# Linear attention and a gated mixture of experts on one core: three copies of v and one clamp of k done by GpSimd

## The chip, the core and the metric

The kernel runs on one core of a Trainium2 chip. The metric is the device time of one execution in microseconds (us); less is better. Engines: TensorE (PE, matrix products and transposes; PEld is its weight load), VectorE (DVE), ScalarE (ACT), GpSimd (POOL) and SyncE (SP, which here only starts transfers). Each engine works its own instructions off in order, and semaphores order the engines against each other.

## The reference

Two stages, batch 8, 8 heads, 576 positions, head width 64 (so 512 model columns), 8 experts of width 1024:

```
phi(x) = where(x > 0, x, exp(x) - 1) + 1
q_p, k_p = phi(q), phi(k)
kv  = einsum('bhsd,bhse->bhde', k_p, v);  z = sum(k_p, over s)
out = einsum('bhsd,bhde->bhse', q_p, kv) / (einsum('bhsd,bhd->bhs', q_p, z) + 1e-6)
x   = out with the heads side by side                       # 8 x 576 x 512
logits = x @ w_gate;  local = sigmoid(x @ w_local)
for each batch, position by position:
    e = argmax(logits[s]) if s == 0 or local[s] < 0.5 else the previous position's e
    out[s] = softmax(logits[s])[e] * (relu(x[s] @ w1[e]) @ w2[e])
```

## The kernel before

**Tiling.** Each batch a is cut into two groups n = 2a, 2a + 1 of four heads. A group's k, q and v are tiles of 128 rows by 1152 floats (`kraw`, `qraw`, `vraw`; four, two and three buffers taken in turn). Positions lie 9 to a row; the first ninth is handled apart as the "last" slice.

**Steps of a group n.** `Lk.n`, `Lq.n`, `Lv.n` load (on SP's queue; for n = 0 and 1 v comes in two parts, `Lv.n` with 5 of the 9 columns and `Lv.n.1` with 4). `E.k.n` and `E.q.n` are the exponentials on ACT. phi of k is `min(max(k + 1, 1), exp(k))` for batch 0: `CL.n` is the clamp `max(k + 1, 1)` into a spare tile, `P.k.n` takes the minimum in DVE. phi of q is `E2.q.n` (relu, in place) and `P.q.n` (min and add, in two halves). `VC.n` and `VC.n.1` copy v into `vone`, which has a column of ones beside each 64 columns so that one product yields both kv and z. `K.n` and `K.n.1` are those products on PE, `KC.n` copies their result `kv` out of PSUM. `QL`/`Q` transpose q on PE, `QLC`/`QC` copy that out to `qT`. `NL`/`N` form numerators and denominators, `DL`/`D` divide on DVE into `xb`, `XL`/`X` transpose that, `XLC`/`XC` copy it to `xT`.

**Steps of a batch a.** `R.a.0` and `R.a.1` are the gate's logits, `PK`/`BK` pick the expert, `W.a.x` loads its weights (transfers started by POOL, since their address comes from the picked index), `H.a.m`/`HC` the hidden layer, `O.a.i`/`OC` the output, `ST` its store. The kernel assumes that one expert serves a whole batch; flags checked at the end start a general path if not (it does not run here).

**Order.** A single hand-written list, `ORDER`, sets the order for all engines: each engine's queue is that list, filtered to its own steps. A number behind a slash is the PSUM slot (`K.1/3` and `K.0/3` share one, so `K.0` needs `KC.1` done). A `^` sends a copy to the engine other than its default: the copies of v go to DVE by default, and with `^` to ACT. So before the change `VC.1`, `VC.1.1` and `VC.0` are ACT's, `VC.0.1` and both clamps DVE's. POOL has, at the start, a few memsets, the identity matrices (`ident`, `identb`) and two small loads; then nothing until `W.0.0`.

**Waits that matter here.** `Lq.2` overwrites the buffer that `P.q.0` reads, so SP holds it until `P.q.0` is done; `Lk.3`, `Lk.2`, `Lq.3` (which waits for `P.q.1`), `Lv.3` (which waits for `VC.0`) and `Lv.2` follow in SP's queue. The clamp of group 0 is put into `vraw[2]`, that of group 1 into `kraw[2]`. On ACT, `E.k.3` stands ahead of `XLC.0`.

Of the kernel before, what the change touches and what calls it, by code (L numbers as in the profile page):

```python
# [20 lines left out]


ORDER = """
Lq.0 Lk.1 FILL/0 Lv.1 Lv.1.1 Lv.0 Lk.0 Lq.1 Lv.0.1 E0.0 P0.0 E.k.1 CL.1 WT/1 E.q.0 P.k.1 QL.0/2 VC.1^
E2.q.0^ QLC.0 K.1/3 VC.1.1^ P.q.0.0 K.1.1 E.k.0 P.q.0 CL.0 Q.0/2 Lq.2 VC.0^ Lk.3 P.k.0 E.q.1 Lk.2 KC.1^
VC.0.1 QC.0 K.0/3 E2.q.1^ K.0.1 P.q.1.0 KC.0^ P.q.1 E.q.2 NL.0/2 N.0.0.1/3 DL.0 Lq.3 E.k.3 Lv.3 WG D.0.0.1
XL.0/2 Lv.2 Q.1/1 XLC.0^ R.0.0/2 QC.1 N.0.0.0/3 RC.0.0 D.0.0.0 W.0.0 E.k.2 N.0.1.1/2 N.0.1.0/1 PK.0 E2.k.3
D.0.1.1 E.q.3 D.0.1.0 BK.0 P.k.3 VC.3^ W.0.1 X.0.0/3 X.0.1/2 XC.0.0 XC.0.1^ K.3/1 E2.q.2^ E2.q.3^ R.0.1/3
# [47 lines left out]
def kernel(  # L76
# [11 lines left out]
    nc = tc.nc  # L88
    P = 128
    B, H, S, Dh = q.shape  # L90
    D = H * Dh
    E = moe_w_gate.shape[1]
# [28 lines left out]
    with ExitStack() as main:  # L121
# [7 lines left out]
        kraw = [raw.tile([P, 2, C, Dh], F32, name=f"kraw{i}") for i in range(NKR)]  # L129
# [71 lines left out]

        BK = 512
        got, other = {}, set()

        def bank(label, *name, dt=F32):
            i = got[name]
            ps = psp.tile([P, SLOTS[i], BK if dt == F32 else 2 * BK], dt, name=label, tag=f"ps{i}")
            ps = open_[name] = ps if size[name] == 2 else ps[:, 0, :]
            return ps
# [51 lines left out]
        def clamp(n):  # L261

            return (kraw[2] if n else vraw[2]).rearrange("p g c d -> p (g c d)")

        def clamp_k(n):
            nc.vector.tensor_scalar(clamp(n), kraw[n].rearrange("p g c d -> p (g c d)"), 1.0, 1.0,
                                    Alu.add, Alu.max)

        def phi(n, x, both=False, c0=0, c1=C, gs=(0, 1)):
# [18 lines left out]
        def on_act(*name, act=False):  # L288
            return (name in other) != act

        def copy(dst, src, *name, act=False):
            (nc.scalar.copy if on_act(*name, act=act) else nc.vector.tensor_copy)(dst, src)  # L292

        def v_ones(n, i=None):
            c0, c1 = (0, C) if i is None else CV[i:i + 2]
            dst, src = vone[n % 2][:, :, c0:c1, :Dh], vraw[n % NV][:, :, c0:c1, :]
            copy(dst, src, *(("VC", n) + ((i,) if i else ())))
# [11 lines left out]
        def kv_out(n):  # L309
            kv[n] = kvp.tile([P, 2, W], F32, name="kv")  # L310
            copy(kv[n], open_.pop(("K", n))[:, :, :W], "KC", n)
# [8 lines left out]
        def q_main_out(n):  # L320
            ps = open_.pop(("Q", n))
            for r in range(2):
                copy(qT[n][:, :, :SM].rearrange("q t (i p r) -> q r t i p", i=NC - 1, r=2)[:, r],
                     ps[:, r, :].rearrange("q (i t p) -> q t i p", i=NC - 1, t=2), "QC", n, act=True)
# [319 lines left out]
        for a in range(B):  # L644
            for j in range(NJ):
                n = a * NJ + j
# [7 lines left out]
                for x in "kq":  # L654
                    both = a > 0 or x == "q"
                    if not both:
                        op(("CL", n), lambda n=n: clamp_k(n))
                    c0 = int(a == 0 and x == "q")
                    if c0:
                        if n == 0:  # L660
                            op(("E0", n), exp0)
                            op(("P0", n), phi0)
                    op(("E", x, n), lambda n=n, x=x, c0=c0: exps(n, x, False, c0))
                    if both:
                        op(("E2", x, n), lambda n=n, x=x, c0=c0: relus(n, x, c0))
                    if c0:
                        op(("P", x, n, 0), lambda n=n: phi(n, "q", True, 1, C, (0,)))
                    op(("P", x, n),
                       lambda n=n, x=x, b=both, c0=c0: phi(n, x, b, c0, C, (1,) if c0 else (0, 1)))
# [59 lines left out]
        for word in ORDER.split():  # L729
            name, _, at = word.rstrip("^").partition("/")  # L730
            name = tuple(int(x) if x.isdigit() else x for x in name.split("."))
# [261 lines left out]
```

## Time and profile before

| | |
|---|---|
| time, median of 3 runs | 220.41 us (218.78 to 221.2) |
| the profiled execution's own time | 222.17 us |
| its span in the profile | 220.6 us |
| mean granted TensorE clock | 0.971 |
| busy: PE, DVE, ACT, POOL | 207.2 (94%), 177.8 (81%), 131.2 (59%), 13.6 us (6%) |
| chain that ended last, by engine | PE 87%, DMA 5%, DVE 2%, ACT 2%, issue 1% |

The profile is of one execution, and its times count from the start of the span; 1.57 us of the execution's time lie outside of it. The page cuts the span into 40 slices: there PE is at nine tenths or more in every slice from the sixth to the last but one, and lower in the first five; the DMA engines are at nine tenths or more in the slices 2 to 7. POOL is busy in slices 1 and 5 and after that only in short pieces.

### The profile page before, as it was taken

What the parts mean: (1) busy time and instruction counts of PE and PEld (TensorE: products, weight loads), DVE (VectorE), ACT (ScalarE), POOL (GpSimd) and SP (SyncE); (2) the same over time, 40 slices, a digit from 0 to 9 for tenths busy, and PEclk for the clock granted to TensorE, in tenths of its full rate; (3) what the DMA queues carried; (4) which work ended last, traced back from release to release, by engine and by line L of the source; (5) the groups of instructions that cost most, each with busy time, mean ns of one, the idle gap of its engine ahead of it and who ended that gap; (6) DMA issues with size and microseconds to landing.
All of it is one profiled execution on the core that took longest, in us unless ns stands there. A gap on an engine that the chain in (4) does not pass through costs nothing.

```text
span 220.6 us, 8567 instructions
## 1 busy us (share of the span) xinstructions
PE 207.2 (94%) x3702; PEld 152.7 (69%) x3715; DVE 177.8 (81%) x459; ACT 131.2 (59%) x197; POOL 13.6 (6%) x41
## 2 busy tenths in 40 slices
PE   7886699999999999999999999999999999999990
PEld 2575578767886698875888568874889578647640
DVE  0794987698999999999999989779897989586730
ACT  2678727599999999795248984483753302501120
POOL 4000500000010000210000000110000001100000
PEclk9978879999999999999999999999999999999997
DMA  5999999896976798999359979599230008998043
GB/s 192 369 307 341 166 195 216 270 371 222 360 249 260 236 378 235 370 228 195 67 154 332 304 232 333 97 183 155 77 146 3 4 15 324 189 197 255 3 153 97
DMA packets 24447, 46.77 MB, mean 212 GB/s; under 512 B 2124, under 2 KB 9808, under 8 KB 23508
## 3 DMA queue, kind: packets, MB, share of 16 engines
q1 hardware_dynamic: 16324, 37.49, 49.1%
q0 software_dynamic: 7392, 8.41, 24.0%
q8 instruction: 31, 0.51, 1.0%
q10 hardware_dynamic: 688, 0.26, 0.5%
q14 instruction: 12, 0.10, 0.1%
HBM read 61.88 MB, written 9.44 MB: 323 GB/s over the span
## 4 chain that ended last, share of the span: by engine, by line
PE 87%; DMA 5%; DVE 2%; ACT 2%; issue 1%; SPq 0%; DVEq 0%; ACTq 0%
PE hps L556 29%; PE yps L578 25%; PE kvps L306 9%; PE nps L357 7%; PE tq L317 6%; DMA kraw<-in_k_dram 5%; PE yps L582 4%; PE tx L391 3%; PE lps L433 2%; ACT ek L241 1%; PE npl L376 1%; PE lps L427 1%; PE tql L330 1%; DVE xb L345 1%; DVE kraw L274 1%
## 5 line engine op out<-in xcount | busy, mean ns | idle before, releaser
L556 PE MATMUL hps<-xT,w1cur 128*128 128x288 bf16 x512 | 67.8, 288 | 0.0
L578 PE MATMUL yps<-w2cur,hT 128*128 128x512 bf16 x243 | 58.4, 379 | 0.7
L556 PEld LDWEIGHTS <-w1cur 128*128 128x128 bf16 x512 | 49.1, 98 | 13.3 <-issue 0.6
L565 ACT ACTIVATE hT<-hps 128x576 bf16<-128x576 f32 x41 | 26.7, 657 | 37.7 <-PE hps L556 28.8
L578 PEld LDWEIGHTS <-hT 128*128 128x128 bf16 x256 | 24.0, 98 | 25.5 <-issue 0.3
L306 PE MATMUL kvps<-vone,kraw 64*64 64x65 f32 x1152 | 21.8, 229 | 2.0 <-ACT vone L292 1.0
L345 DVE TENSOR_TENSOR xb<-nps,rec 128x512 bf16<-128x512 f32 x32 | 22.1, 691 | 1.1
L281 DVE SCALAR_TENSOR_TENSOR fq<-fq,qraw 128x576 f32<-128x576 f32 (+1 forms) x32 | 22.4, 741 | 0.2
L306 PEld LDWEIGHTS kvps<-vone,kraw 64*64 64x64 f32 x1152 | 19.7, 143 | 3.6 <-ACT vone L292 1.5
L274 DVE SCALAR_TENSOR_TENSOR kraw<-ek,kraw 128x1152 f32<-128x1152 f32 x14 | 18.8, 1346 | 2.1 <-ACT kraw L248 2.1
L567 DVE TENSOR_SCALAR hT<-hps 128x576 bf16<-128x576 f32 x23 | 17.1, 752 | 4.2 <-PE hps L556 4.0
L357 PE MATMUL nps<-kv,qT 64*64 64x65 f32 x1024 | 20.3, 228 | 0.0
L241 ACT ACTIVATE fq<-qraw 128x1152 f32<-128x1152 f32 (+1 forms) x16 | 18.4, 1153 | 2.8 <-DMA qraw<-in_q_dram 2.8
L241 ACT ACTIVATE ek<-kraw 128x1152 f32<-128x1152 f32 x16 | 18.8, 1173 | 2.3 <-DMA kraw<-in_k_dram 2.3
L357 PEld LDWEIGHTS nps<-kv,qT 64*64 64x64 f32 x1024 | 18.2, 143 | 1.2 <-issue 0.5
L593 ACT ACTIVATE yo<-yps,pr 128x512 f32<-128x512 f32 x16 | 11.0, 690 | 11.3 <-PE yps L578 11.2
L317 PE MATMUL tq<-ident,fq 128*128 128x128 f32 x128 | 17.3, 280 | 0.0
L292 ACT COPY qT<-tq 128x512 f32<-128x512 f32 x28 | 15.9, 644 | 0.7 <-PE tq L317 0.6
L317 PEld LDWEIGHTS tq<-ident,fq 128*128 128x128 f32 x128 | 15.0, 145 | 0.8
L292 ACT COPY xT<-tx 128x1024 bf16<-128x1024 bf16 x9 | 9.1, 1014 | 10.7 <-PE tx L391 10.7
L595 DVE TENSOR_SCALAR yo<-yps,pr 128x512 f32<-128x512 f32 x16 | 11.7, 744 | 2.0 <-PE yps L578 1.9
L248 ACT ACTIVATE kraw<-kraw 128x1152 f32<-128x1152 f32 x10 | 11.7, 1169 | 0.0
(108 smaller groups left out, 218.5 us busy)
## 6 DMA issues: line engine op xcount, KB each, us to landing
kraw<-in_k_dram SPq DMA_DIRECT2D x16, 576.0 KB, 7.2
qraw<-in_q_dram SPq DMA_DIRECT2D x14, 576.0 KB, 5.3
vraw<-in_v_dram SPq DMA_DIRECT2D x14, 576.0 KB, 5.5
w1s<-in_moe_w_dram POOLq DMA_DIRECT2D x7, 1024.0 KB, 11.3
w2s<-in_moe_w_dram POOLq DMA_DIRECT2D x7, 1024.0 KB, 13.1
out_dram<-yo SPq DMA_DIRECT2D x14, 512.0 KB, 5.1
qraw<-in_q_dram SPq DMA_DIRECT2D x2, 512.0 KB, 4.0
w2cur<-in_moe_w_dram POOLq DMA_DIRECT2D x1, 1024.0 KB
```

The source lines that it names most:

```text
L241: nc.scalar.activation(e[:, :, c0:c1, :], raw_, Act.Exp)
L274: nc.vector.scalar_tensor_tensor(r, e, 1.0, r, Alu.min, Alu.add)
L281: nc.vector.scalar_tensor_tensor(e[:, g], e[:, g], 1.0, r[:, g], Alu.min, Alu.add)
L292: (nc.scalar.copy if on_act(*name, act=act) else nc.vector.tensor_copy)(dst, src)
L306: nc.tensor.matmul(ps[g * PH:(g + 1) * PH, t, :W], lhsT=f[h, g, c, :], rhs=vo[h, g, c, :], start=(c == 0), stop=(c == C - 1))
L317: nc.tensor.transpose(ps[:, r, i * P:(i + 1) * P], ex_[n, "q"][:, 1 + i + (NC - 1) * r, :, :], identity=ident)
L345: nc.vector.tensor_tensor(dst, ps[:, :, :, :Dh].rearrange("p g (i t) e -> p g i t e", t=2), rec.rearrange("p g (i t o) -> p g i t o", t=2, ...
L357: nc.tensor.matmul(ps[o * PH:(o + 1) * PH, g, (il * 2 + t) * W:(il * 2 + t + 1) * W], lhsT=qT[n][g * PH:(g + 1) * PH, t, i * P + o * PH:i ...
L556: nc.tensor.matmul(ps[:, u, :HS], lhsT=w1b[:, kk, m * P:(m + 1) * P], rhs=xT[b][:, kk, u * HS:(u + 1) * HS], start=(kk == 0), stop=(kk == ...
L565: nc.scalar.activation(dst, src, Act.Relu)
L567: nc.vector.tensor_scalar(dst, src, 0.0, None, Alu.max)
L578: nc.tensor.matmul(ps, lhsT=hT[b][:, m, i * P:(i + 1) * P], rhs=w2b[:, m, :], start=(m == 0), stop=(m == FK - 1))
```

## The change

Three of the four copies of v of batch 0 (`VC.1`, `VC.1.1`, `VC.0`) go from ACT to GpSimd, and the second clamp of batch 0 (`CL.0`, of k of group 0) from DVE to GpSimd. Their places in `ORDER` stay.

```
-... QL.0/2 VC.1^
-E2.q.0^ QLC.0 K.1/3 VC.1.1^ P.q.0.0 K.1.1 E.k.0 P.q.0 CL.0 Q.0/2 Lq.2 VC.0^ Lk.3 ...
+... QL.0/2 VC.1
+E2.q.0^ QLC.0 K.1/3 VC.1.1 P.q.0.0 K.1.1 E.k.0 P.q.0 CL.0 Q.0/2 Lq.2 VC.0 Lk.3 ...
...
+        on_pool = {("VC", 1), ("VC", 1, 1), ("VC", 0), ("CL", 0)}
...
         def clamp_k(n):
-            nc.vector.tensor_scalar(clamp(n), kraw[n].rearrange("p g c d -> p (g c d)"), 1.0, 1.0,
+            (nc.gpsimd if ("CL", n) in on_pool else nc.vector).tensor_scalar(clamp(n), kraw[n].rearrange("p g c d -> p (g c d)"), 1.0, 1.0,
                                     Alu.add, Alu.max)
...
         def copy(dst, src, *name, act=False):
-            (nc.scalar.copy if on_act(*name, act=act) else nc.vector.tensor_copy)(dst, src)
+            (nc.gpsimd.tensor_copy if name in on_pool else
+             nc.scalar.copy if on_act(*name, act=act) else nc.vector.tensor_copy)(dst, src)
```

ACT's queue at the start of batch 0, before. `vone_78<-vraw_75` are the two parts of `VC.1`, `vone_77<-vraw_74` is `VC.0`; `fq` is `E.q`, `ek` is `E.k`, `kv` is `KC.1`:

```order
L241 ACTIVATE ek<-kraw_69 128x1152
L241 ACTIVATE fq<-qraw_72 128x2x8x64
L292 COPY vone_78<-vraw_75 128x2x5x64
L292 COPY qT<-tql 128x2x64 x2
L292 COPY vone_78<-vraw_75 128x2x4x64
L241 ACTIVATE ek<-kraw_68 128x1152
L292 COPY vone_77<-vraw_74 128x2x5x64
L241 ACTIVATE fq<-qraw_73 128x2x8x64
L292 COPY kv<-kvps 128x130
```

The same place of ACT's queue of the change (line numbers are one or two higher there):

```order
L242 ACTIVATE ek<-kraw_69 128x1152
L242 ACTIVATE fq<-qraw_72 128x2x8x64
L293 COPY qT<-tql 128x2x64 x2
L242 ACTIVATE ek<-kraw_68 128x1152
L242 ACTIVATE fq<-qraw_73 128x2x8x64
L293 COPY kv<-kvps 128x130
```

The three copies are gone from it and nothing else has moved.

POOL's queue at the same place, before: the last of the constants, then the index that picks the expert, and the weights of batch 0:

```order
masks.py:199 AFFINE_SELECT ident<-ident 128x128
L223 MEMSET age 1x1 x3
L186 CAST identb<-ident 128x128
L481 TENSOR_LOAD i_408
L499 ISA
L499 DMA w1cur<-in_moe_w_dram 128x4x256
```

And of the change:

```order
masks.py:199 AFFINE_SELECT ident<-ident 128x128
L224 MEMSET age 1x1 x3
L293 COPY vone_78<-vraw_75 128x2x5x64
L186 CAST identb<-ident 128x128
L293 COPY vone_78<-vraw_75 128x2x4x64
L267 TENSOR_SCALAR vraw_76<-kraw_68 128x1152
L293 COPY vone_77<-vraw_74 128x2x5x64
L483 TENSOR_LOAD i_408
L501 ISA
L501 DMA w1cur<-in_moe_w_dram 128x4x256
```

`VC.1` stands ahead of the cast of the identity, `VC.1.1`, `CL.0` and `VC.0` behind it, all ahead of the weights.

DVE's queue, before. `kraw_70<-kraw_69` is `CL.1`, `vraw_76<-kraw_68` is `CL.0`; the minimum behind each is `P.k`:

```order
L266 TENSOR_SCALAR kraw_70<-kraw_69 128x1152
L276 TENSOR_TENSOR kraw_69<-kraw_70,ek 128x1152
L252 TENSOR_SCALAR qraw_72<-qraw_72 128x2x512
L281 SCALAR_TENSOR_TENSOR fq<-fq,qraw_72 128x8x64 x2
L266 TENSOR_SCALAR vraw_76<-kraw_68 128x1152
L276 TENSOR_TENSOR kraw_68<-vraw_76,ek 128x1152
L292 COPY vone_77<-vraw_74 128x2x4x64
```

And of the change:

```order
L267 TENSOR_SCALAR kraw_70<-kraw_69 128x1152
L277 TENSOR_TENSOR kraw_69<-kraw_70,ek 128x1152
L253 TENSOR_SCALAR qraw_72<-qraw_72 128x2x512
L282 SCALAR_TENSOR_TENSOR fq<-fq,qraw_72 128x8x64 x2
L277 TENSOR_TENSOR kraw_68<-vraw_76,ek 128x1152
L293 COPY vone_77<-vraw_74 128x2x4x64
```

One clamp is gone; `P.k.0` now waits for POOL's.

More of the change, by code (lines that the diff above doesn't have):

```diff
@@ L23 @@
 ORDER = """
-Lq.0 Lk.1 FILL/0 Lv.1 Lv.1.1 Lv.0 Lk.0 Lq.1 Lv.0.1 E0.0 P0.0 E.k.1 CL.1 WT/1 E.q.0 P.k.1 QL.0/2 VC.1^
-E2.q.0^ QLC.0 K.1/3 VC.1.1^ P.q.0.0 K.1.1 E.k.0 P.q.0 CL.0 Q.0/2 Lq.2 VC.0^ Lk.3 P.k.0 E.q.1 Lk.2 KC.1^
+Lq.0 Lk.1 FILL/0 Lv.1 Lv.1.1 Lv.0 Lk.0 Lq.1 Lv.0.1 E0.0 P0.0 E.k.1 CL.1 WT/1 E.q.0 P.k.1 QL.0/2 VC.1
+E2.q.0^ QLC.0 K.1/3 VC.1.1 P.q.0.0 K.1.1 E.k.0 P.q.0 CL.0 Q.0/2 Lq.2 VC.0 Lk.3 P.k.0 E.q.1 Lk.2 KC.1^
 VC.0.1 QC.0 K.0/3 E2.q.1^ K.0.1 P.q.1.0 KC.0^ P.q.1 E.q.2 NL.0/2 N.0.0.1/3 DL.0 Lq.3 E.k.3 Lv.3 WG D.0.0.1
```

## The prediction

> **What bounds the kernel now.** I first cut the span where the hidden layer of batch 0 begins, at 28.7 us, and asked for the busy time of each engine in the two pieces. The columns are PE, PEld, DVE, ACT, POOL, then the granted clock, the DMA share and GB/s.
>
> ```profile
> 0.00:28.70 28.70, 21.57 (x452) 15.93 (x453) 18.61 (x43) 18.56 (x26) 5.60 (x20) 0.85 0.90 270
> 28.70:219.60 190.90, 185.64 (x3256) 136.82 (x3266) 159.14 (x417) 112.66 (x171) 7.96 (x21) 0.99 0.73 204
> ```
>
> Behind 28.7 us PE is busy 185.64 of 190.90 us: a start that comes later by one microsecond ends later by one. Ahead of it PE stands still for 7.1 us, and the change lies wholly there. So the question is what sets 28.7. The chain that ended last, for that piece (start, length, what):
>
> ```profile
> 1.50 5.63 DMA kraw<-in_k_dram
> ...
> 7.16 1.16 ACT ek L241
> 8.32 0.95 ACT fq L241
> 9.27 0.63 ACT vone L292
> 9.94 2.27 PE kvps L306 x72
> 12.22 6.26 DMA kraw<-in_k_dram
> 18.58 1.16 ACT ek L241
> 19.75 0.27 ACT xT L292
> 20.06 0.31 PE lps L427 x8
> ...
> 28.88 3.17 PE hps L556 x19
> ```
>
> Read it backwards. From 18.58 on the steps hand over to one another: `E.k.3`, `XLC.0` behind it in ACT's queue, the logits `R.0.0`, the numerators and divisions of batch 0, `P.k.3`, `K.3`, the hidden layer. `E.k.3` starts when k of group 3 has landed, at 18.48. The upper part would make the copy `VC.1` (L292) a link, by way of `K.1` on PE to the load at 12.22. I do not believe that link: `Lk.3` overwrites the tile with the raw gate weights, whose transposes were over long before `K.1`. SP's own waits (total, times, longest) and its timeline name another:
>
> ```profile
> SPq L139 <- DVE fq L281: 7.8, 2, 5.9
> 11.67 0.37 SPq L139 DMA_DIRECT2D qraw<-in_q_dram  x1
> 12.22 1.89 SPq L139 DMA_DIRECT2D kraw<-in_k_dram  x2
> ```
>
> SP sat for 5.9 us on `P.q.0` (L281), then issued `Lq.2` at 11.67 and, 0.55 us later in the same queue, `Lk.3`. So the true chain of the start goes through DVE:
>
> ```profile
> 8.35 1.36 DVE L276 TENSOR_TENSOR kraw<-kraw,ek 128x1152 f32<-128x1152 f32 x1 [0.44 <-ACT ek L241]
> 9.63 0.69 DVE L252 TENSOR_SCALAR qraw<-qraw 128x1024 f32<-128x1024 f32 x1
> 10.35 1.29 DVE L281 SCALAR_TENSOR_TENSOR fq<-fq,qraw 128x512 f32<-128x512 f32 x2
> 11.56 0.75 DVE L266 TENSOR_SCALAR vraw<-kraw 128x1152 f32<-128x1152 f32 x1
> 12.49 1.36 DVE L276 TENSOR_TENSOR kraw<-vraw,ek 128x1152 f32<-128x1152 f32 x1 [0.17 <-ACT ek L241]
> 13.76 0.42 DVE L292 COPY vone<-vraw 128x512 f32<-128x512 f32 x1
> ```
>
> `P.k.1`, `E2.q.0` and the two halves of `P.q.0` run without a gap from 8.35 to 11.64; `P.q.0`'s end releases `Lq.2`. Little else is in flight then: in the next two rows (columns as above) the DMA falls to 158 and 173 GB/s.
>
> ```profile
> 12.00:13.00 1.00, 1.00 (x12) 0.91 (x5) 0.82 (x2) 1.00 (x3) 0.00 (x0) 0.50 0.96 158
> 13.00:14.00 1.00, 0.80 (x5) 0.56 (x4) 1.00 (x2) 1.00 (x3) 0.00 (x0) 0.81 0.59 173
> ```
>
> So what delays DVE between 8.35 and 11.64 delays the end of the kernel, and what frees ACT there does not hasten it.
>
> **What is removed.** ACT loses its three copies (the rows are below), 0.71 + 0.63 + 0.71 = 2.05 us. Hidden: ACT waits for k3 at 18.58 whatever it did before. What it brings is `KC.1` 0.6 us earlier, and with it `K.0`, which waited for it:
>
> ```profile
> 14.23 1.28 PE L306 MATMUL kvps<-vone,kraw 64*64 64x65 f32 x72 [0.43 <-ACT kv L292]
> 17.55 1.09 PE L317 MATMUL tq<-ident,fq 128*128 128x128 f32 x8
> ```
>
> `K.0` could start at 13.9, when `P.k.0` is done (12.49 + 1.36): 0.3 us. But PE's last step before `R.0.0` is `Q.1`, ended at 18.64, and `R.0.0` starts at 20.06 when `XLC.0` is through: 1.42 us of slack already, so 0.3 more bring 0. DVE loses `CL.0`, 0.75 us; `P.k.0` waits for `E.k.0` anyway (the 0.17 in its row): 0. The gain is 0 to 0.3 us; I take 0.
>
> **What is added: the price of the GpSimd work.** The page of before has no large GpSimd copy. The nearest rows are its cast of 128 columns and its copy of one element, and, for another engine, the ACT groups of these very copies (count, busy us, mean ns):
>
> ```profile
> 3.48 0.29 POOL L186 CAST identb<-ident 128x128 bf16<-128x128 f32 x1
> 39.29 0.18 POOL L492 COPY seen<-w2cur 1x1 bf16<-1x1 bf16 x1 [13.97 <-DMA w2cur<-in_moe_w_dram]
> L292 ACT COPY vone<-vraw 128x640 f32<-128x640 f32 x2 | 1.4, 710 | 0.0
> L292 ACT COPY vone<-vraw 128x512 f32<-128x512 f32 x1 | 0.6, 630 | 0.0
> ```
>
> (0.29 - 0.18) / 127 is 0.87 ns per column: 0.18 + 640 x 0.87 ns = 0.73 us for `VC.1` and `VC.0`, 0.62 for `VC.1.1`, 1.18 for `CL.0`, if its two operations cost no more than a copy. Below, DVE's 0.75 for the clamp; above, twice my figures, since a line through 1 and 128 columns is stretched nine times. I take the line, which ACT's rows match. The Trainium skill ("GPSIMD Engine Reference", Engine selection) puts one-input work on GpSimd at "roughly line-rate", but its Key points make VectorE about twice as fast for elementwise work; by the second, `VC.1.1` would be 0.84 (an estimate, twice DVE's 0.42 at 13.76) and the sum below larger by about a third.
>
> **What is added: DVE and GpSimd at the same time.** GpSimd's small copy `seen` takes 0.18 us in five of its seven places. The other two:
>
> ```profile
> 60.52 1.35 DVE L274 SCALAR_TENSOR_TENSOR kraw<-ek,kraw 128x1152 f32<-128x1152 f32 x1
> 60.83 1.08 POOL L492 COPY seen<-w2s 1x1 bf16<-1x1 bf16 x1
> 61.79 0.75 DVE L252 TENSOR_SCALAR qraw<-qraw 128x1152 f32<-128x1152 f32 x1
> ...
> 107.92 1.42 DVE L281 SCALAR_TENSOR_TENSOR fq<-fq,qraw 128x576 f32<-128x576 f32 x2
> 108.90 0.48 POOL L492 COPY seen<-w2s 1x1 bf16<-1x1 bf16 x1 [14.45 <-DMA w2s<-in_moe_w_dram]
> ```
>
> It ends at 61.91 and 109.38, 0.04 us behind a DVE instruction with two inputs in SBUF (61.87, 109.34): GpSimd's read was held until that was over. `P.k.1` and `P.q.0` are such instructions. What the rows don't show is the reverse, a long GpSimd read that holds DVE. I take the holding to be mutual, each waiting for the other's instruction to end and taking turns, because `seen` got in at 61.87 though DVE's next instruction (61.79) stood ready. The Trainium skill says it outright ("SBUF — State Buffer", Who interferes with whom): a DVE instruction with two SBUF inputs, or in its fast two-port mode, and a GpSimd one that reads SBUF exclude each other, and whichever starts first keeps the other out for its whole length. The rows alone would also allow GpSimd to be the only loser; that would make of my +2.0 a +0 to +1.0.
>
> **The sum.** When does `VC.1` start? By the issues and landings of v's parts (the first row is three issues, 0.5 to 0.6 us apart; last column: us to landing):
>
> ```profile
> 2.00 1.79 SPq L139 DMA_DIRECT2D vraw<-in_v_dram x3
> vraw<-in_v_dram SPq DMA_DIRECT2D x1, 320.0 KB, 6.1
> vraw<-in_v_dram SPq DMA_DIRECT2D x1, 256.0 KB, 6.4
> 11.29 1.17 ACT L241 ACTIVATE ek<-kraw 128x1152 f32<-128x1152 f32 x1 [0.55 <-DMA kraw<-in_k_dram]
> ```
>
> v of group 1 is there at 8.1 and about 8.9; k of group 0 at 11.26. DVE is idle for 0.44 us ahead of `P.k.1` (its row above), so `VC.1` gets in at 8.15, just ahead of `P.k.1`.
> - `VC.1` first: `P.k.1` loses 0.53 (8.35 to 8.88); then, a turn each, the cast of the identity 0.29 (it stands behind `VC.1` now), `VC.1.1` 0.62, `CL.0` 1.18. Together 2.62: `P.q.0` ends at 14.26.
> - `P.k.1` first: 0.73 + 0.29 + 0.62 = 1.64, and `CL.0` falls behind `P.q.0`, which ends at 13.28.
>
> `Lk.3` goes 0.58 behind that. It took 6.26 us to land; the first k, issued when little was in flight as this one would be, took 5.63. So k3 lands later by 2.6 or 2.0 in the first case, 1.6 or 1.0 in the second. I choose 2.0: the first order, by v's landing, and the shorter transfer, since the DMA has nearly run dry by 14.
>
> The new wait is `P.k.0`'s for `CL.0`. Queued behind it on DVE are `VC.0.1`, `E2.q.1`, `P.q.1` and the first division; `K.0`, `Q.1` and (through `P.q.1`) `Lq.3` wait for those. `VC.0` may slip in too: 14.26 + 0.73 + 1.36 puts `K.0` at 16.4 instead of 14.23, 2.2 us later, against 1.42 of slack plus the 2.0 by which `R.0.0` itself moves. Hidden; without k3's delay it would cost 0.8. `Lv.3`, which waits for `VC.0` now on GpSimd, stands behind `Lq.3` and loses nothing of its own. GpSimd's index load is reached by 16, with its weights issued at 22 or later: 0.
>
> Everything from `E.k.3` on moves by 2.0. The span becomes 222.6, the profiled execution's time 224.2. That execution was 1.76 us above the median of its runs, so I put the shift on the median: 220.4 + 2.0 = **222.4 us**, with 221.4 to 223.4 as this case's own range.
>
> **Rivals.**
> - *GpSimd at twice the price.* The turns then cost 1.3 + 0.3 + 1.2 + 2.4 = 5.2 on `P.q.0`, and 4.6 to 5.2 at the end: about 225.2. For it: the stretched line. Against it: the match with ACT's rows.
> - *GpSimd alone waits.* DVE runs on, k3 lands on time, but the copies run after 11.64: `VC.1`, cast, `VC.1.1` and `CL.0` end at about 14.5, `P.k.0` at 15.9, `VC.0` by 16.6; `K.0` starts up to 2.4 us late, 1.0 beyond its slack. 220.4 to 221.4. For it: the two rows show only this direction.
> - *Not slower: no holding at all.* `VC.1` is done at 8.9, `K.1` starts at `P.k.1`'s end, `CL.0` ends at 12.45, just when `E.k.0` does, and `K.0` gains 0.3. Since k3 lands as before, at most 0.3 comes of it: 220.1. It decides as soon as DVE's stretch still ends by 11.64. For a gain of over 1% k3 would have to land over 2.2 us earlier, and nothing that `P.q.0` needs comes sooner. Against it: the two `seen` rows.
> - *The change does nothing it says* is out: the four instructions stand in GpSimd's queue.
>
> **How the numbers follow.** Turn-taking 0.50, GpSimd alone waits 0.27, not slower 0.11, twice the price 0.12. The range: below, the not-slower case less half a microsecond of scatter between runs, 219.8; above, the double price, 225.2. A measurement here tells about 1% from no change, 2.2 us. Over 1% slower: the double price and nearly half of turn-taking (its upper part, 2.2 to 2.6, and scatter), 0.12 + 0.24 = 0.36. Over 1% faster: only by scatter or something I don't see, 0.04. Within: 0.60.
>
> **What would show it.** GpSimd's rows: 0.73, 0.62, 1.18, 0.73 us, or longer where they wait. DVE's `P.k.1`: a start near 8.9 or a length over 1.36; `P.q.0`'s end between 13.3 and 14.3, `Lq.2` right behind it, `E.k.3` near 20.6, the first hidden product near 30.9. I am wrong in the mechanism if `P.q.0` still ends at 11.6, and in the link to the end if `Lk.3` is issued late and the hidden layer still starts at 28.9.

## The result: slower by 2.8%, above the range

The change takes 227.12 us (median of four executions, 226.56 to 227.86) against 220.2 us for the kernel before on the same chip: a ratio of 1.028, 95% interval 1.0237 to 1.0323, so about 6 us (the two medians by themselves lie 6.9 us apart). The prediction was 222.4 us with a range to 225.2. The profiled executions, 226.99 and 222.17 us, differ by 4.82 us, since that of before lay above its median; the two traces explain these 4.82 us. Where the executions of one kernel fall into a faster and a slower group, as those of `copies_only` below, its ratio goes by the faster group.

The same two pieces as before, cut where the hidden layer of batch 0 begins, now at 34.5 us (columns as in the prediction):

```profile
0.00:34.50 34.50, 21.77 (x451) 16.31 (x452) 22.29 (x41) 16.95 (x23) 13.74 (x24) 0.80 0.75 223
34.50:225.40 190.90, 184.84 (x3258) 136.26 (x3267) 159.62 (x418) 112.75 (x171) 7.94 (x21) 0.99 0.73 205
```

From TensorE's first hidden product to the end of the span it is 190.8 us (225.4 - 34.56), and 191.9 us before (220.6 - 28.74): the stretch behind is no longer than it was, 1.0 us shorter even. The whole loss lies ahead of it, where that product starts 5.82 us later. GpSimd's and VectorE's timelines of the change at the start of batch 0 (start, length, what):

```profile
8.20 0.72 POOL L293 COPY vone<-vraw 128x640 f32<-128x640 f32 x1 [4.67 <-DMA vraw<-in_v_dram]
8.87 1.41 POOL L186 CAST identb<-ident 128x128 bf16<-128x128 f32 x1
10.24 1.06 POOL L293 COPY vone<-vraw 128x512 f32<-128x512 f32 x1
11.35 4.45 POOL L267 TENSOR_SCALAR vraw<-kraw 128x1152 f32<-128x1152 f32 x1
15.77 0.81 POOL L293 COPY vone<-vraw 128x640 f32<-128x640 f32 x1
...
8.38 1.76 DVE L277 TENSOR_TENSOR kraw<-kraw,ek 128x1152 f32<-128x1152 f32 x1 [0.44 <-ACT ek L242]
10.05 0.78 DVE L253 TENSOR_SCALAR qraw<-qraw 128x1024 f32<-128x1024 f32 x1
10.87 5.13 DVE L282 SCALAR_TENSOR_TENSOR fq<-fq,qraw 128x512 f32<-128x512 f32 x2
15.92 1.87 DVE L277 TENSOR_TENSOR kraw<-vraw,ek 128x1152 f32<-128x1152 f32 x1
```

`CL.0` takes 4.45 us on GpSimd; it took 0.75 on VectorE. The two halves of `P.q.0` start at 10.87 and end at 16.00, 5.13 us instead of 1.29: the second half ends only 0.20 us behind the clamp, which is over at 15.80. What follows, on SyncE, ScalarE and TensorE:

```profile
16.03 0.37 SPq L139 DMA_DIRECT2D qraw<-in_q_dram  x1
16.58 0.88 SPq L139 DMA_DIRECT2D kraw<-in_k_dram  x2
...
21.56 1.15 ACT L242 ACTIVATE ek<-kraw 128x1152 f32<-128x1152 f32 x1
25.12 0.37 ACT L293 COPY xT<-txl 128x256 bf16<-128x256 bf16 x1 [2.40 <-PE txl L404]
...
16.15 1.94 PE L319 MATMUL tq<-ident,fq 128*128 128x128 f32 x8 [3.80 <-DVE fq L282]
18.05 2.23 PE L308 MATMUL kvps<-vone,kraw 64*64 64x65 f32 x72
20.65 0.71 PE L378 MATMUL npl<-kv,qT 64*64 64x65 f32 x16 [0.38 <-ACT kv L293]
21.14 0.84 PE L359 MATMUL nps<-kv,qT 64*64 64x65 f32 x18
24.41 0.46 PE L359 MATMUL nps<-kv,qT 64*64 64x65 f32 x14 [2.43 <-issue]
26.45 0.39 PE L429 MATMUL lps<-wg,xT 128*64 128x9 bf16 x8
34.56 1.63 PE L558 MATMUL hps<-xT,w1cur 128*128 128x288 bf16 x12
```

`Lq.2` leaves right behind `P.q.0`, at 16.03 instead of 11.67. But `E.k.3` (21.56) no longer waits for a transfer; `XLC.0` waits for TensorE. The limit has changed hands. Read TensorE's starts against those of before: `Q.0` +4.05 (16.15, was 12.10); `NL.0` +4.75, with `K.0` 0.95 longer at a granted clock of 0.5 (1.0 before); `R.0.0` +6.39, behind a stop of 2.43 us among the numerators for which the profile shows no wait ("issue"); the hidden layer +5.82.

### The profile page after: what moved, and what is told of

Same layout as the page of the kernel before. It is cut to its first block, busy times and chain, and to the rows that moved or that the text cites. A ratio compares the mean times of both kernels' runs of the same rounds, so it can differ in the third digit from the quotient of the medians.

```text
span 225.4 us, 8568 instructions
## 1 busy us (share of the span) xinstructions
PE 206.6 (92%) x3702; PEld 152.6 (68%) x3715; DVE 181.9 (81%) x458; ACT 129.7 (58%) x194; POOL 21.7 (10%) x45
## 4 chain that ended last, share of the span: by engine, by line
PE 75%; DMA 9%; DVE 5%; ACT 4%; issue 3%; SPq 1%; POOLq 0%; DVEq 0%
PE hps L558 25%; PE yps L580 22%; PE kvps L308 7%; PE nps L359 6%; PE tq L319 6%; DMA w1s<-in_moe_w_dram 5%; DMA kraw<-in_k_dram 3%; PE yps L584 3%; DVE fq L282 2%; PE tx L393 2%; PE npl L378 1%; SPq L139 1%; PE lps L435 1%; PE lps L429 1%; DVE kraw L275 1%
## 5 line engine op out<-in xcount | busy, mean ns | idle before, releaser
L558 PE MATMUL hps<-xT,w1cur 128*128 128x288 bf16 x512 | 67.0, 286 | 0.0
L282 DVE SCALAR_TENSOR_TENSOR fq<-fq,qraw 128x576 f32<-128x576 f32 (+1 forms) x32 | 26.2, 863 | 0.2
L319 PE MATMUL tq<-ident,fq 128*128 128x128 f32 x128 | 18.1, 289 | 3.8 <-DVE fq L282 3.8
L242 ACT ACTIVATE fq<-qraw 128x1152 f32<-128x1152 f32 (+1 forms) x16 | 18.5, 1158 | 1.6 <-DMA qraw<-in_q_dram 1.5
L319 PEld LDWEIGHTS tq<-ident,fq 128*128 128x128 f32 x128 | 15.5, 149 | 4.7 <-issue 4.0
L505 POOL DMA_DIRECT2D w1s<-in_moe_w_dram x7 | 2.7, 383 | 96.4 <-DMA w1s<-in_moe_w_dram 31.6
```

The lines of the kernel that those rows point to most:

```text
L242: nc.scalar.activation(e[:, :, c0:c1, :], raw_, Act.Exp)
L282: nc.vector.scalar_tensor_tensor(e[:, g], e[:, g], 1.0, r[:, g], Alu.min, Alu.add)
L319: nc.tensor.transpose(ps[:, r, i * P:(i + 1) * P], ex_[n, "q"][:, 1 + i + (NC - 1) * r, :, :], identity=ident)
L558: nc.tensor.matmul(ps[:, u, :HS], lhsT=w1b[:, kk, m * P:(m + 1) * P], rhs=xT[b][:, kk, u * HS:(u + 1) * HS], start=(kk == 0), stop=(kk == ...
```

## The experiments

Two theories after the result. **Price:** the clamp's 4.45 us, through `P.q.0`, is nearly the whole loss, and with the assumed 1.18 us the sum would have come out. **Something besides:** the copies and the unexplained stop cost of their own. In all the ratios, the kernel before is run on the same chip.

### One part alone

`copies_only` leaves the clamp on VectorE, `clamp_only` the copies on ScalarE:

```
 copies_only:  on_pool = {("VC", 1), ("VC", 1, 1), ("VC", 0)}
 clamp_only:   on_pool = {("CL", 0)}     # VC.1^ VC.1.1^ VC.0^ as before
```

> The three copies of v on GpSimd, the clamp CL.0 back on VectorE. Theory A (the clamp alone makes the loss: 4.45 us on GpSimd, and the second half of P.q.0 held for all of it): P.k.1 is stretched to about 1.76 us as in the change, P.q.0 ends at 12.2 to 12.5 instead of 16.0, and the time is 0 to 0.8 us above before. Theory B (turn-taking of all four instructions makes it): P.q.0 ends at 13 or later and 3 us or more of the loss of 6.9 us stay.

> The clamp CL.0 alone on GpSimd, the copies of v back on ScalarE. Theory A: the clamp takes about 4.4 us again. If it gets in between the halves of P.q.0 the second half is held and the time is 5 to 7 us above before; if P.q.0 is through first, Lq.2 goes out on time at 11.7, but P.k.0 starts at 16.1 instead of 12.5, K.0 with it, and the time is 2 to 3 us above. Theory B: the clamp costs its line of 1.2 us when no copies stand ahead of it, P.k.0 starts by 13, and the time is within 1 us of before.

`clamp_only`: ratio 1.0178 (1.0077 to 1.028). Its rows:

```profile
10.77 1.29 DVE L282 SCALAR_TENSOR_TENSOR fq<-fq,qraw 128x512 f32<-128x512 f32 x2
11.53 4.49 POOL L267 TENSOR_SCALAR vraw<-kraw 128x1152 f32<-128x1152 f32 x1 [7.75 <-DMA kraw<-in_k_dram]
16.05 1.36 DVE L277 TENSOR_TENSOR kraw<-vraw,ek 128x1152 f32<-128x1152 f32 x1 [3.99 <-POOL vraw L267]
```

The clamp came behind `P.q.0` here, so the loads left on time (12.09), and still it costs some 4 us: `P.k.0` waits 3.99 us for it, and `K.0` starts at 17.52. The price is paid by way of `K.0` if not by way of `P.q.0`.

`copies_only`: ratio 1.0106 (1.0 to 1.0212), the single times lying near 224 (three) and near 228 (three); the rows are of one that took 228.15. `P.q.0` ends at 13.06, as the second theory had it (13 or later), the time, some 2.3 us above before, lies between the two, and the stop is there without the clamp:

```profile
10.32 2.19 POOL L293 COPY vone<-vraw 128x512 f32<-128x512 f32 x2
10.96 2.10 DVE L282 SCALAR_TENSOR_TENSOR fq<-fq,qraw 128x512 f32<-128x512 f32 x2
21.00 0.70 PE L359 MATMUL nps<-kv,qT 64*64 64x65 f32 x14 [2.63 <-issue]
```

`VC.1.1` and `VC.0` together take 2.19 us, and `P.q.0` beside them 0.81 more than alone. The two ratios add up to the change's (1.06% + 1.78% = 2.84%), but each is known to about one per cent only.

The scatter of `copies_only` raised the question whether the stop makes it; one more execution of the same kernel:

> The same kernel as copies_only, whose six runs fell into two groups, near 224.3 and near 228.3 us, and whose trace, of a run of 228.15, has a stop of 2.6 us in PE at 18.4. If the stop makes the groups, a run near 224 has none of it, and one near 228 has it. If both have it, the groups come from elsewhere.

It gave 225.59 us with a stop of 2.12 us. So the stop does not by itself make the scatter, and what does stays open.

### The disputed costs by themselves

`probe` runs GpSimd's and VectorE's instructions ahead of the kernel, alone and against each other (its total says nothing):

```
 nc.gpsimd.tensor_copy(d0, s0);  nc.gpsimd.tensor_scalar(d0, s0, 1.0, 1.0, Alu.add, Alu.max);  ...
 nc.vector.tensor_scalar(v1[:, :8], d0[:, :8], 0.0, None, Alu.max)     # beside a clamp
 3 x nc.gpsimd.tensor_copy(vone, qraw) beside 3 x nc.vector.tensor_tensor(v1, s0, s1, min)
```

> The kernel before with a row of instructions on constant tiles ahead of it, which delays all the rest: its total time says nothing, its first rows do. GpSimd alone: copies of 128x640 and 128x1152, the clamp 128x1152 (add and max), the same with one operation, the clamp at 128x512. If the clamp's price is GpSimd's own, it takes 4.4 us alone; if the turns with VectorE made it long, it takes 1.2 us alone. Then a clamp on GpSimd with, on VectorE a little later, an instruction with two SBUF inputs, and in a second piece one with a single input in its fast form: held to the clamp's end, or running at their 0.65 and 0.69 us. Last, three copies on GpSimd and three minima on VectorE side by side: turns show as 0.73 and 1.36 us each with waits in between.

GpSimd alone: two copies, the clamp, one of its two operations alone, and the clamp on 512 columns:

```profile
3.03 0.71 POOL L749 COPY vone<-kraw 128x640 f32<-128x640 f32 x1
7.62 1.14 POOL L750 COPY kraw<-kraw 128x1152 f32<-128x1152 f32 x1 [3.43 <-DVE kraw L747]
8.98 4.10 POOL L751 TENSOR_SCALAR kraw<-kraw 128x1152 f32<-128x1152 f32 x1
13.16 3.13 POOL L752 TENSOR_SCALAR kraw<-kraw 128x1152 f32<-128x1152 f32 x1
19.58 1.92 POOL L754 TENSOR_SCALAR kraw<-kraw 128x512 f32<-128x512 f32 x1
```

A copy of 1152 columns is 1.14 us, close to the prediction's line (1.18); arithmetic with one constant is 2.7 times, the clamp with two 3.6 times that. VectorE alone, then both at once:

```profile
33.22 1.35 DVE L768 TENSOR_TENSOR qraw<-kraw,kraw 128x1152 f32<-128x1152 f32 x1
34.63 5.36 POOL L771 COPY vone<-qraw 128x640 f32<-128x640 f32 x3 [3.40 <-DVE qraw L768]
34.48 4.93 DVE L773 TENSOR_TENSOR vraw<-kraw,kraw 128x1152 f32<-128x1152 f32 x3
...
21.47 4.09 POOL L756 TENSOR_SCALAR vraw<-kraw 128x1152 f32<-128x1152 f32 x1
21.53 4.05 DVE L757 TENSOR_SCALAR vraw<-kraw 128x8 f32<-128x8 f32 x1 [10.36 <-POOL kraw L754]
```

Three minima that take 3 x 1.35 = 4.05 alone take 4.93, three copies of 0.71 take 5.36: the holding goes both ways, in turns. Even a VectorE operation with one input on 8 columns, issued 0.06 us behind a clamp, ended with it, 4.05 us later.

### The change with a clamp at the assumed price

In `copy_for_clamp` GpSimd does `CL.0` as a copy, and VectorE takes `k + 1` in `P.k.0`, which leaves out the maximum with 1:

```
-            nc.gpsimd.tensor_scalar(clamp(0), k0, 1.0, 1.0, Alu.add, Alu.max)
+            nc.gpsimd.tensor_copy(clamp(0), k0)
-            nc.vector.tensor_tensor(r, clamp(0), e, op=Alu.min)
+            nc.vector.scalar_tensor_tensor(r, clamp(0), 1.0, e, Alu.add, Alu.min)
```

> The change, but GpSimd only copies k where it clamped, and P.k.0 on VectorE adds the 1 and takes the minimum in its one instruction (for k below 0 that leaves out the clamp to 1). GpSimd's instruction of 1152 columns stays in its place and costs 1.14 us instead of 4.10, about the 1.18 that the prediction had put on it. If the mis-sized clamp is the prediction's one error, P.q.0 ends at 13.3 to 14.3 and the time is 1.0 to 2.6 us above before. If more than that went wrong, the time stays 4 us or more above.

```profile
11.25 1.51 POOL L268 COPY vraw<-kraw 128x1152 f32<-128x1152 f32 x1
10.78 2.53 DVE L288 SCALAR_TENSOR_TENSOR fq<-fq,qraw 128x512 f32<-128x512 f32 x2
21.73 0.46 PE L365 MATMUL nps<-kv,qT 64*64 64x65 f32 x14 [2.42 <-issue]
```

`P.q.0` ends at 13.31, almost exactly the lower of the prediction's two sums (13.28). That is in part luck: here `VC.1` went first and the copy got in between the halves of `P.q.0`, which is the order of the higher sum (14.26). But the time is 1.0197 of before (1.0108 to 1.0285), 4.3 us (2.4 to 6.3) where the sum says 2.0, and the stop is there. So the price alone hardly settles it.

### What the stop is

The profile's list of DMA queues names two "instruction"; one of them, q8, moves packets of 16 KB (0.02 MB), 31 in an execution. Each stop ends 2.1 to 2.7 us behind such a packet: in the change the packet moves at 21.8 and TensorE goes on at 24.41, in `copies_only` at 18.4 and 21.00. That suggests that TensorE has run out of program. The list shows when a packet moves, not when it is asked for or for which engine; these are inferred. Every kernel with the stop has its copies of v on GpSimd; with the copies on ScalarE none shows among the first numerators, neither before nor in `clamp_only`, whose `Q.0` starts at 12.52 and whose packet comes at 12.2, ahead of it. Why it comes so much earlier there is not shown. In the change the packet moves in the midst of the burst that `P.q.0` let go (three loads of 576 KB at 408 GB/s, last column):

```profile
16.00:17.00 1.00, 0.85 (x4) 0.88 (x5) 1.00 (x2) 0.00 (x0) 0.58 (x1) 0.50 0.00 0
19.00:20.00 1.00, 1.00 (x48) 1.00 (x40) 1.00 (x2) 0.29 (x1) 0.00 (x0) 0.50 1.04 408
```

**The order of the loads.** The load of k of group 3 put ahead of that of q of group 2, with `E.q.2` behind `XLC.0`, in the kernel before (`k3_first`, measured twice) and in the change (`change_k_first`, with `Lk.2` moved up too):

```
-... P.q.0 CL.0 Q.0/2 Lq.2 VC.0^ Lk.3 P.k.0 ...  P.q.1 E.q.2 NL.0/2 ...  XLC.0^ R.0.0/2
+... P.q.0 Lk.3 CL.0 Q.0/2 Lq.2 VC.0^ P.k.0 ...  P.q.1 NL.0/2 ...  XLC.0^ E.q.2 R.0.0/2
```

> The kernel before with one load moved: Lk.3 ahead of Lq.2 in SP's queue (it then waits only for the transposes of the gate weights, over at 8.6), and E.q.2 behind XLC.0 on ScalarE. If the landing of k3 sets the start, as the prediction says, XLC.0 no longer waits for it, the logits R.0.0 start when Q.1 ends, at about 18.7 instead of 20.06, and the time falls by about 1.4 us. If the start hangs on something else, the time stays within 0.4 us.

> The change with Lk.3 and Lk.2 ahead of Lq.2 in SP's queue and E.q.2 behind XLC.0 on ScalarE. k3 and k2 then go out near 8.7 and 10.2, before P.q.0 is done, and only q2 is left to start at 16.0. If the stop of 2.4 us in PE (21.98 to 24.41) comes from the fetch of its instructions behind the burst of three loads, it shrinks or goes, R.0.0 starts near 24 instead of 26.45, and the time falls by 2 to 2.5 us against the change. If the landing of k3 were still what sets the start, the time would fall as well, but the stop would stay. If neither matters, it stays within 0.5 us of the change: about 227.

`k3_first`: 0.9972 (0.9939 to 1.0005). The hidden layer started 1.4 us earlier in the profile, and little of it was left at the end. `change_k_first`: 1.0226 (1.0133 to 1.0318); one load alone leaves behind `P.q.0` now, the packet comes at 19.4, the stop among the first numerators is gone and `R.0.0` starts at 23.78. But the next packet (26.2) is late in its turn:

```profile
28.72 0.21 PE L359 MATMUL nps<-kv,qT 64*64 64x65 f32 x1 [2.21 <-issue]
```

**Where the program is cut.** Other fills of TensorE at the start move its packets' boundaries:

```
 change_more_fills:  fills = {("WT",): 19}                        # 15 in the change
 change_pad, copy_for_clamp_pad, copies_pad, before_pad:
     fills = {("WT",): 13}  and 33 fills of 32 x 32 instead of 9
```

> The change with 19 instead of 15 fill products ahead of the gate's transposes: PE's program is eight instructions longer ahead of the stop. If the stop is a fetch of instructions at a fixed place in PE's program, it comes eight instructions earlier in the work: in front of or within the first numerators (2 of them in the trace instead of 18). If it is a wait for data, it stays behind the 18th.

> The change with 24 more of the smallest products (32x32, on zeros) at PE's start and two fewer of the large ones: PE's program is 44 instructions longer ahead of all real work, in time that PE spends waiting for its first data anyway. Theory F (the stop of 2.4 us in the first numerators is a fetch of PE's instructions, asked for only when PE gets past Q.0's wait, and queued behind the three loads that the same P.q.0 releases): the request now falls ahead of that wait, into K.1.1, the packet comes by 13 instead of 21.8, the stop is gone, R.0.0 starts near 24.2 instead of 26.45, and the time falls by 1.5 to 2.5 us to about 225. Theory D (the stop is a wait for data that the trace doesn't show): it stays behind the 18th product and the time stays near 227.

> copy_for_clamp (GpSimd copies k where it clamped, P.k.0 adds the 1) with the same padding of PE's program. Theory F: no stop at 19.3, R.0.0 near 21.5 instead of 23.7, and the time is 1.0 to 2.6 us above before, which is what the prediction's sum gave for the price that it assumed. Theory D: 4 us above before, as without the padding.

> copies_only (the three copies of v on GpSimd, the clamp on VectorE) with the same padding. Theory F: no stop at 18.4, the spread of its runs narrows, and the time is 0.5 to 1.5 us above before instead of 2.3 and more. Theory D: no change.

> The kernel before with the same padding of PE's program, as a control: its packet comes at 12.2 and PE has no stop there, so the padding should change nothing, within 0.5 us. If the padding itself is worth 1 us or more, the three others have to be read against this one.

`change_more_fills` said nothing on the boundary: the turns fell otherwise, `P.q.0` ended at 12.38 ahead of the clamp, no stop came, and one execution took 229.2 us, with `P.k.0` waiting as in `clamp_only`. In the three padded kernels the packet came at 12.0 to 12.4 and the first numerators ran without a stop, `R.0.0` at 23.80, 21.01 and 21.13, near what was expected. The times were 1.0209 (1.0134 to 1.0284), 1.0148 (1.0084 to 1.0211) and 1.0146 (1.0086 to 1.0205), the last two above the 1.0 to 2.6 and 0.5 to 1.5 us that were expected. In these profiles the hidden layer starts earlier than without the padding (32.69, 30.47 and 29.75 us), but from there to the end they take 194.0 to 195.5 us (190.8 in the change, 191.9 before), with new stops of 1.52, 1.52 and 1.24 us between 71 and 74 us. The control spoils the reading of the times: `before_pad` has a ratio of 1.0207 (1.0125 to 1.029), but its executions spread from 221.53 to 227.34 us, and the profiled one, 221.53, is no slower than the kernel before beside it (220.17 to 222.0). What spreads them is not shown. So the padding shows that the stop hangs on where the program is cut, and not what it costs.

**The loads out of the way, TensorE's program unchanged.** `change_later_loads` and `copy_for_clamp_later_loads` put one small transfer ahead of `Lq.2`, `change_loads_last` two, one after the other; the `q_buffer` kernels load q of group 2 into memory that is idle until the first outputs, so `Lq.2`, `Lk.3` and `Lk.2` don't wait for `P.q.0`:

```
+ LATE:   nc.sync.dma_start(out=late, in_=ex_[0, "q"][0:1, 1, 1, 0:1])    # reads what P.q.0 writes
+ LATE2:  nc.sync.dma_start(out=late2, in_=late)                          # loads_last only
  q_buffer:
+ q2own = yp.tile([P, NC - 1, D], F32, name="yo")...
+ qbuf = lambda n: q2own if n == 2 else qraw[n % NQR]
```

> The change with one transfer of 4 bytes ahead of the load of q of group 2 in SyncE's queue, which reads one element that P.q.0 writes; so the three loads leave about 0.75 us later, and TensorE's program is unchanged. If the stop of 2.43 us is TensorE's instruction fetch behind those loads: the first 16 KB packet of the instruction queue comes within about 1 us of the start of Q.0 (near 17 instead of 21.8), the first numerators of the second numerators' row run without a stop of over 1 us, R.0.0 starts near 24 (26.45 in the change), and the time is 1.5 to 2.5 us under the change, near 225 us (224.3 to 225.8). If the stop has another cause, it stays, and the time is that of the change or 0.5 us above it (226.5 to 228).

> The same small transfer ahead of the loads, in the kernel where GpSimd copies k instead of clamping it (VectorE then takes k plus 1 in P.k.0, so the clamp to 1 for negative k is left out). If the fetch theory holds: the packet comes near 14.5 instead of 19.2, no stop of over 1 us, R.0.0 near 21.3 (23.72 without the small transfer), and the time is 1.0 to 2.6 us above the kernel before, which is what the prediction's sum gives for a clamp at its assumed price. If not: the stop stays, and the time is 3.5 to 5 us above the kernel before.

> The change with q of group 2 loaded into memory that is idle until the first outputs, so that the load and the two behind it in SyncE's queue no longer wait for P.q.0; TensorE's program is unchanged, and Q.0 still waits for P.q.0 (start near 16.15). If the stop is the fetch behind the loads: the loads are over, or nearly, when TensorE gets past Q.0's wait, the packet comes 2.8 to 3.3 us after it (19.0 to 19.5, was 21.8), the stop of 2.43 us falls to 0.5 or less, R.0.0 starts near 24 (26.45 in the change), and the time is 1.5 to 3 us under the change (224 to 225.5). If the fetch takes 5.5 us whatever the loads do: packet near 21.7, the stop stays, R.0.0 near 26.4, and the time is that of the change (226 to 228).

> The same buffer in the kernel where GpSimd copies k instead of clamping it (VectorE takes k plus 1 in P.k.0, so the clamp to 1 for negative k is left out). Q.0 starts near 13.45. Fetch behind the loads: packet between 16.3 and 17.5 (19.2 without the buffer; some loads still run then), a stop of 1 us or less instead of 2.42, R.0.0 near 21.5 to 22.3 (23.72), and the time 1.5 to 3.5 us under copy_for_clamp, that is 1 to 2.6 us above the kernel before. Otherwise: packet near 19, stop stays, time 3.5 to 5 us above the kernel before.

> The change with two small transfers, the second of what the first brings, ahead of the load of q of group 2: the three loads leave 2.5 to 3 us later than in the change (near 18.9), and their data moves from about 20.8. Fetch behind the loads: it now reaches the transfer engines ahead of them, the packet comes near 19.0 to 19.5 instead of 21.8, and the first numerators run without a stop over 0.5 us; R.0.0 near 24; the time then depends on what the late loads cost elsewhere (224.5 to 228). Otherwise: packet near 21.7 and the stop stays.

All by the profiles (us; the packets by windows of 0.2; "later" is the time from `P.q.0`'s end to `Lq.2`, which is 0.03 otherwise):

| kernel | loads behind `P.q.0` | `Q.0` starts | packet | between | first stop | hidden layer | ratio to before |
|---|---|---|---|---|---|---|---|
| the change | 3 | 16.15 | 21.8 | 5.6 | 2.43 | 34.56 | 1.028 |
| `change_later_loads` | 3, 0.9 later | 16.32 | 21.8 | 5.5 | 2.70 | 35.10 | 1.041 (1.0333 to 1.0486) |
| `change_loads_last` | 3, 2.4 later | 15.75 | 18.6 | 2.9 | none | 33.50 | 1.0272 (1.0207 to 1.0337) |
| `change_q_buffer` | none | 16.31 | 19.0 | 2.7 | 0.16 | 34.08 | 1.0251 (1.0199 to 1.0302) |
| `copy_for_clamp` | 3 | 13.45 | 19.2 | 5.8 | 2.42 | 31.83 | 1.0197 |
| `copy_for_clamp_later_loads` | 3, 0.9 later | 13.59 | 19.0 | 5.4 | 2.85 | 33.25 | 1.0239 (1.0173 to 1.0305) |
| `copy_for_clamp_q_buffer` | none | 13.72 | 16.8 | 3.1 | none | 30.66 | 1.0113 (1.0064 to 1.0162) |

The `later_loads` pair failed against my expectation: the packet hardly moved, the stop stayed, and `change_later_loads` took longer (1.041) than its rows explain. The next three say why. With the transfer engines empty (the row is `change_q_buffer` from 18 to 19 us) the packet still takes 2.7 us from `Q.0`'s start; it then moves alone:

```profile
18.00:19.00 1.00, 1.00 (x31) 0.82 (x33) 0.97 (x3) 0.72 (x2) 0.00 (x0) 0.50 0.00 0
...
DMA packets 1, 0.02 MB, mean 82 GB/s; under 512 B 0, under 2 KB 0, under 8 KB 0
...
q8 instruction: 1, 0.02, 29.5%
```

In `change_later_loads` the loads' data moves from 18.5 on (69 GB/s, and 318 from 19.0 to 19.5), so they are ahead of a packet due at 19.0; loads 2.4 us later are behind it. The theory of the fetch held on both sides, with loads early and with loads late: with the copies on GpSimd and no padding the packet comes 2.7 to 3.1 us behind `Q.0`'s start when little is in flight, 5.4 to 5.8 when three loads are ahead of it (5.2 in `copies_only`). Its effect on the time did not come as expected. In `change_q_buffer` the next boundary pays, its packet (26.2) standing, it seems, behind `Lq.3` and the loads of v:

```profile
21.56 0.46 PE L362 MATMUL nps<-kv,qT 64*64 64x65 f32 x14 [0.16 <-issue]
28.69 0.21 PE L362 MATMUL nps<-kv,qT 64*64 64x65 f32 x1 [2.97 <-issue]
```

In `change_loads_last` no stop is left, and the late loads cost as much: `E.q.2` waits for q, `XLC.0` stands behind it, and the logits for that:

```profile
24.94 0.30 PE L431 MATMUL lps<-wg,xT 128*64 128x9 bf16 x8 [1.95 <-ACT xT L295]
```

In `copy_for_clamp_q_buffer`, with the assumed price and no first stop, the time falls to where the prediction's sum put it: 1.0113, 2.5 us above before (1.4 to 3.6); the predicted 2.0 us lie inside. That is no proof of the sum's path: here `Lk.3` and `Lk.2` leave from 8.68 on and wait for `P.q.0` no longer, so its delay can't reach the end by k3's landing, as it does in the sum; and a later stop of 1.68 us, up to 25.27, is left. Against `copy_for_clamp` the intervals overlap, so the gain is likely but not proven.

### A version ahead of both

> The kernel before with the load of k of group 3 ahead of that of q of group 2, and E.q.2 behind XLC.0, measured once more (0.9972 of the kernel before, 0.9939 to 1.0005, so far). If the earlier first numerators are worth anything by the end: 0.5 to 1.5 us under the kernel before with an interval below 1. If what is won there is given back at later fetches and waits: within 0.5 us of it, and the interval holds 1.

The second measurement of `k3_first` gives 0.9949 (0.991 to 0.9988), about 1.1 us under the kernel before, with the first piece 1.4 us shorter:

```profile
8.64 0.37 SPq L139 DMA_DIRECT2D kraw<-in_k_dram  x1
19.05 0.30 PE L427 MATMUL lps<-wg,xT 128*64 128x9 bf16 x8
27.36 0.88 PE L556 MATMUL hps<-xT,w1cur 128*128 128x288 bf16 x3
```

`Lk.3` leaves at 8.64 instead of 12.22. Of the two measurements one interval just reaches 1, the other doesn't.

## Why the prediction was wrong, point by point

- **What bounds the kernel:** right. Behind the first hidden product nothing was lost, and what delays VectorE between 8.35 and 11.64 delays the end. That k's landing set the first logits is borne out by `k3_first`, where `R.0.0` came 1.0 us earlier.
- **What is removed:** ScalarE's relief shows no gain in the rows, as predicted: `KC.1` came 0.29 us earlier (0.6 expected), and `K.0` stood behind `Q.0`. No run tried it alone.
- **The price of the GpSimd work: the step that failed.** The line through a cast and a copy was right for the copies (0.72 and 0.81 us for 0.73; 1.14 alone for 1152 columns) and wrong for `CL.0`: 1.18 us assumed, 4.10 alone and 4.45 in the kernel. The condition I wrote myself, "if its two operations cost no more than a copy", was the one that broke, and the upper end, twice the line, did not bracket it either: the clamp is 3.5 times the line. The "roughly line-rate" that the Trainium skill ("GPSIMD Engine Reference", Engine selection) gives for one input fits the copies (1.14 us for 1152 columns) and not the clamp (4.10).
- **VectorE and GpSimd at the same time:** right, and mutual. The probe shows turns both ways, `P.k.1` lost 0.40 us (0.53 expected), the cast waited (1.41 for 0.29), and the second half of `P.q.0` was held until about the clamp's end. The Trainium skill ("SBUF — State Buffer", Who interferes with whom) agrees: the tiny operation on 8 columns, held for 4.05 us, is the whole-instruction lock that it describes.
- **The sum:** with a clamp at about the assumed price `P.q.0` ended at 13.31 (13.28 or 14.26 expected, the lower by another order than the one that came); with the real one at 16.00. The loads followed `P.q.0` as said, 4.36 us late.
- **What is late next:** missed. I let k3's landing carry the shift and left TensorE's own chain 1.42 us of slack. At 4 us of delay that slack is used up: `Q.0`, `K.0` at half the granted clock and the numerators set `XLC.0`, while `E.k.3` waited for nothing.
- **Not in the sum at all:** TensorE's program, which by the inference above is fetched behind the loads. In the change this is a stop of 2.43 us. What it adds to the time there is not settled: the cures that took it away moved the ratio to between 1.0209 and 1.0272, each interval overlapping the change's; a later stop or the late loads took its place.
- **The rivals:** "twice the price" was the nearest, and its 225.2 us still too low; the three other rivals are out by the rows.

## What to carry over

Price an operation on an engine by a row of the same operation: a copy says nothing about arithmetic, and one isolated measurement of it costs little. When an instruction that lets loads go becomes late, follow everything that waits for it, not only the first load: the engine that reads its result, and whatever else must pass through the same transfer engines. A stop without a shown wait is worth looking up in the list of the DMA queues.

## What the runs showed of the hardware that I had not expected

- GpSimd takes 4.10 us for an add and a maximum on 128 x 1152 floats, 3.13 for one operation, 1.14 for a copy.
- A packet of what seem to be TensorE's instructions (16 KB) seems to queue with the kernel's own loads: with the copies on GpSimd, 2.7 to 3.1 us from `Q.0`'s start to the packet with little in flight, 5.2 to 5.8 behind 1.77 MB, and 2.1 to 2.7 more until TensorE goes on. In the kernel before, where the packet came at 12.2, no stop shows.
- With 22 more pairs of instructions at TensorE's start (24 small fills more, two large ones fewer) the executions of the kernel before spread from 221.53 to 227.34 us, a ratio of 1.0207 (1.0125 to 1.029).
